# The last pass of a decode-layer gradient kernel, put into written order on each engine

## The chip, the cores and the metric

The kernel runs on one core of a Trainium2 chip. The metric is the device time of one execution in microseconds (us); less is better. "Before" is the kernel as it stands, "after" the kernel with the change. Engines are named as in the profile: PE (matmul; PEld is its weight load), DVE (vector), ACT (scalar), POOL and SP. POOL and SP mostly issue DMAs here.

## What is computed

Two decode steps of a layer pair run one after the other on a single token and share all weights and caches: grouped-query attention over a cache of 65,536 positions, then a two-layer perceptron with a squared ReLU. The kernel returns the output and the gradients of everything.

```python
x = x + A(layernorm(x), k_cache, v_cache, wq, wo)   # 4 KV groups, 8 query heads each, head size 128
x = x + B(layernorm(x), w1, b1, w2, b2)             # relu(x @ w1 + b1) ** 2 @ w2 + b2
x = x + A(layernorm(x), k_cache, v_cache, wq, wo)   # the same caches and weights again
x = x + B(layernorm(x), w1, b1, w2, b2)
out, vjp = jax.vjp(f, ...); grads = vjp(grad_out)   # gradients of x, both caches, wq, wo, w1, b1, w2, b2
```

The caches hold 67 MB each (bf16). Their gradients, as large again, are sums over the two uses, so they can only be written in the last pass, when the scores and the upstream gradients of both uses are known.

## The kernel before

The kernel goes over the caches in four passes: forward attention of the first use, forward of the second, backward of the second (`attn_bwd3`, query gradient only) and a last pass, `attn_bwd4` (line 1050). The last pass does the backward of the first use and writes the cache gradients of both. It takes about the last 765 us of the span and is what the change touches.

**Items and units.** The last pass works on 4 groups of 64 *items*. An item is 8 columns of a group, 8 blocks of 128 positions by 128 numbers, 0.26 MB of K and 0.26 MB of V; it produces as much gradient of each. Four items make a *unit* of 32 columns. For each item i there are these stages:

- `vT` (L1100): 8 PE transposes of V into a PSUM tile `ps_tr`, and one evacuation (copy from PSUM to SBUF by ACT or DVE, lines 155 and 158 in the helper `evac`).
- `vS` (L1123, the "products"): 8 matmuls of the transposed V with the upstream gradients into `ps_sc`. At a unit's first column a matmul subtracts a correction (L1114). At its last column DVE multiplies twice by the exponentials (L1132, L1133), POOL copies twice (L1134, L1135), and the four parts are the tile X.
- `xT_behind` (L1149): once per unit, 8 PE transposes of X and one evacuation.
- `k8`: `dq` (L1166), 8 matmuls of K with X, then `grads` (L1194), two pairs of matmuls, here called A and B. Each fills a `ps_gg` tile with 1,024 fp32 columns, which ACT or DVE evacuates into a staging area. After four items POOL issues the two gradient writes (L1214, L1215).

`ps_tr` and `ps_gg` have two buffers each, `ps_sc` has one.

**Background steps.** A table `bg` holds steps that are due at a loop count. In the last pass they are: row dot products (`dot_va`: a DVE multiply at L433, then an ACT sum at L434 that needs it), which fetch 0.26 MB each; weight gradients; and set-ups of the next group. A weight gradient comes as *rows* steps (L1245 two small DVE casts, L1248 four small matmuls into `ps_gg`, one evacuation) and *out* steps (`outer2`, L1275: two matmuls into `ps_gg`, one evacuation, and per two steps a 0.5 MB write by POOL, L1279). Nearly every loop count from 73 to 226 has one rows or out step: 38 rows and 116 out steps. The rows steps come in five stretches (9, 9, 6, 10 and 4 of them).

**Order.** A scheduler arranges each engine's instructions at build time by priority and its own idea of when their inputs are ready; at run time each engine keeps that order. A helper `in_order` (line 640) runs a step and ties the first instruction that it adds on each engine behind the one written before it on that engine, without a wait between engines; with `each=True` it ties every one. `pipeline` (line 659) walks the loop count i, calls each stage for item i minus its lag, then the background steps of i under `in_order`. In the last pass (line 1232) the stages are free to be moved and of each background step only the first instruction per engine is tied. The opening, up to items 13, 11, 8 and 6 of the stages, is written out by hand and tied instruction by instruction. Which engine takes an evacuation is decided by a running sum of estimated costs at the time the line is written.

K and V tiles are fetched by SP (L284, 1 MB per four items) into a ring of SBUF areas; a fetch waits until the area's last reader on PE is done. An evacuation into a staging area waits until that area's previous write has landed.

Of the kernel before, what the change touches and what calls it, by code (L numbers as in the profile page):

```python
# [18 lines left out]
def kernel(  # L19
# [24 lines left out]
    nc = tc.nc  # L44
    NOSYNC = mybir.DependencyInfo(mybir.DependencyClass.NoSync, mybir.DependencyReason.DATA)
# [21 lines left out]
    UB4 = 512 // R2  # L67
    IPG = C // 8
    TLEAD = 2
# [119 lines left out]
    def part(ap, i, n):  # L189
        return ap[:, i * n:(i + 1) * n]  # L190
# [449 lines left out]
    def in_order(fn, each=False):  # L640

        insts = nc.cur_bb.bb.instructions
        n0 = len(insts)
        before = {}
        fn()
        new = list(insts[n0:])
        want = {i.engine for i in new}
        k = n0 - 1
        while want - set(before) and k >= max(0, n0 - 4000):
            before.setdefault(insts[k].engine, insts[k])  # L650
            k -= 1
        for i in new:
            p = before.pop(i.engine, None)
            if p is not None:
                tc.add_manual_dep(i, p.name, NOSYNC, reason="in_order")
            if each:
                before[i.engine] = i

    def pipeline(n, stages, bg=None, done=()):
        maxlag = max(l for _, l in stages)  # L660
        for i in range(n + maxlag):
            for k, (fn, lag) in enumerate(stages):
                if (done[k] if done else 0) <= i - lag < n:
                    fn(i - lag)
            for fn in (bg or {}).pop(i, ()):
                in_order(fn)
        assert not bg, sorted(bg)

    def items_of(order, turn=0):
# [50 lines left out]
    def attn_fwd(L, order, eT, s_areas, more=None, keep=(), have=(), q_at=(20, 4), narrow=None):  # L720
# [80 lines left out]
        def v8(idx):  # L801
# [9 lines left out]
            if c8 + 8 == C:  # L811
                sl = slice(g * R, (g + 1) * R)
                nc.vector.tensor_tensor(out=L["oT"][:, sl], in0=ps_o[:, :, 0], in1=L["rZ"][:, sl], op=ALU.mult)
                nc.vector.tensor_copy(out=L["oTb"][:, sl], in_=L["oT"][:, sl])

        pipeline(n, [(kT, 0), (kS, TLEAD), (v8, LAGV)], bg)
        return vstream.areas

# [161 lines left out]
    def attn_bwd3(L, og, order, eT, dqT, bg, turn, vhad):  # L980
# [49 lines left out]
        def k8(idx):  # L1030
# [13 lines left out]
            if idx % IPG == IPG - 1:  # L1044
                nc.vector.scalar_tensor_tensor(out=dqT[:, g * R:(g + 1) * R], in0=ps_dq[:, 0, :], scalar=SCALE,
                                               in1=L["rZ"][:, g * R:(g + 1) * R], op0=ALU.mult, op1=ALU.mult)

        pipeline(n, [(vT, 0), (vS, TLEAD), (k8, TLEAD + UB // 8 + 1)], bg)

    def attn_bwd4(La, Lb, oga, ogb, order, eTa, eTb, dqT, bg, group_done, streams, more_stage, tail, KT, vts):  # L1050
        lname = "B1"
        kit = items_of(order)
        n = len(kit)
# [175 lines left out]
        assert len(vts) == 3 and UB4 == 4 * 8  # L1229
        for fn, *args in opening:  # L1230
            in_order(lambda: fn(*args), True)
        pipeline(n, [(vT, 0), (vS, TLEAD), (xT_behind, TLEAD), (k8, TLEAD + UB4 // 8 + 1)], bg, (13, 11, 8, 6))


    def rows_into(rows, cols, nj, twice=False):
# [190 lines left out]
    bg = {}  # L1426
# [136 lines left out]
    stages = Turn([part(e, i, OG) for i in range(2) for e in e_first] + [area[5][:, SLOT - OG:SLOT]])  # L1563
# [31 lines left out]
    bg = {}  # L1595
# [8 lines left out]
    done = [IPG * (j + 1) + LAG4 + 1 for j in range(G)]  # L1604
# [22 lines left out]
    def the_end():  # L1627
        PS["end"] = True
        with tc.high_priority():
# [5 lines left out]
    last_tasks = gwq_tasks(ORD4[-1:], False)  # L1635
    after = [2, 0, 0, 1, 1, 1, 1, 1]
    attn_bwd4(L1, L3, og1, og3, ORD4, eT1, eT3, dqT1, bg, group_done, streams, more_stage,
              lambda i: [t for _, t in zip(range(after[i]), last_tasks)], KT4, vts)
    PS["last"] = True
# [34 lines left out]
```

## Time and profile before

| | before |
|---|---|
| median of 3 runs | 1965.01 us (1962.03 to 1968.48) |
| the profiled execution's own time | 1966.73 us |
| its span | 1965.0 us |
| busy in the span: PE, PEld, DVE, ACT, POOL | 81%, 67%, 56%, 52%, 11% |
| moved by DMA | 802.40 MB, mean 408 GB/s |
| last pass, 1200 to 1965 us: busy PE, DVE, ACT | 619 us, 572 us, 546 us of 765 us |

The span is one execution on the core; the time around it is 1.7 us. "DMA share" is the mean busy share of the core's 16 DMA engines, and "PEclk" the share of full clock that PE was granted. A row of the chain or of the waits gives the engine and line that waited, then what ended the wait.

### The profile page before, as it was taken

What the parts mean: (1) busy time and instruction counts of PE and PEld (TensorE: products, weight loads), DVE (VectorE), ACT (ScalarE), POOL (GpSimd) and SP (SyncE); (2) the same over time, 40 slices, a digit from 0 to 9 for tenths busy, and PEclk for the clock granted to TensorE, in tenths of its full rate; (3) what the DMA queues carried; (4) which work ended last, traced back from release to release, by engine and by line L of the source; (5) the groups of instructions that cost most, each with busy time, mean ns of one, the idle gap of its engine ahead of it and who ended that gap; (6) DMA issues with size and microseconds to landing.
All of it is one profiled execution on the core that took longest, in us unless ns stands there. A gap on an engine that the chain in (4) does not pass through costs nothing. (4 is left out here: it accounts for less than half of the span.)

```text
span 1965.0 us, 65956 instructions
## 1 busy us (share of the span) xinstructions
PE 1582.4 (81%) x30001; PEld 1311.4 (67%) x30052; DVE 1102.6 (56%) x1827; ACT 1028.8 (52%) x1302; POOL 209.5 (11%) x374
## 2 busy tenths in 40 slices
PE   7887887579788866887869888788878688887886
PEld 6887786579788766877868776555555455555553
DVE  4544431046344313746454537687868688776776
ACT  3543433044433322535454437677776677677675
POOL 0000000000000000000000002223222222222222
PEclk9999997669998976899999989899999899999997
DMA  9999999989999999999999999999999999999998
GB/s 395 425 423 421 414 409 404 412 335 421 425 420 420 424 408 391 421 417 419 417 416 402 404 404 409 363 412 420 423 422 422 347 419 422 422 420 421 414 419 328
DMA packets 116227, 802.40 MB, mean 408 GB/s; under 512 B 11484, under 2 KB 11498, under 8 KB 58090
## 3 DMA queue, kind: packets, MB, share of 16 engines
q1 hardware_dynamic: 77530, 612.54, 75.5%
q0 software_dynamic: 30352, 170.94, 21.1%
q10 hardware_dynamic: 8064, 14.68, 2.0%
q8 instruction: 235, 3.85, 0.8%
q14 instruction: 46, 0.38, 0.0%
HBM read 628.18 MB, written 169.95 MB: 406 GB/s over the span
## 5 line engine op out<-in xcount | busy, mean ns | idle before, releaser
L158 DVE COPY small<-ps_tr 128x1024 bf16<-128x1024 bf16 x630 | 427.4, 688 | 315.2 <-PE ps_tr L747 176.5
L155 ACT COPY small<-ps_tr 128x1024 bf16<-128x1024 bf16 x375 | 376.1, 1014 | 360.5 <-PE ps_tr L747 206.9
L155 ACT CAST pair<-ps_gg 128x1024 bf16<-128x1024 f32 (+2 forms) x275 | 264.2, 974 | 119.6 <-PE ps_gg L1194 77.2
L158 DVE CAST pair<-ps_gg 128x1024 bf16<-128x1024 f32 (+1 forms) x209 | 246.8, 1182 | 95.1 <-PE ps_gg L1194 67.1
L747 PE MATMUL ps_tr<-ident_b,pair 128*128 128x128 bf16 x3328 | 252.1, 226 | 38.9 <-DMA pair<-in_A_k_cache_dram 28.3
L1194 PE MATMUL ps_gg<-pair,small 64*128 64x512 bf16 x1024 | 200.1, 399 | 57.1 <-DVE pair L158 15.9
L747 PEld LDWEIGHTS <-pair 128*128 128x128 bf16 x3328 | 201.3, 101 | 44.6 <-DMA pair<-in_A_k_cache_dram 31.8
L809 PE MATMUL ps_acc<-eT,pair 128*128 128x64 bf16 x3840 | 169.3, 205 | 42.8 <-DMA pair<-in_A_v_cache_dram 38.5
L1100 PE MATMUL ps_tr<-ident_b,pair 128*128 128x128 bf16 x2024 | 179.9, 226 | 14.0 <-DVE small L158 5.9
L766 PE MATMUL ps_sc<-L_qpad,small 128*128 128x64 bf16 (+7 forms) x3456 | 174.5, 195 | 18.4 <-ACT small L155 10.9
L809 PEld LDWEIGHTS <-pair 128*128 128x128 bf16 x3840 | 152.9, 104 | 46.3 <-DMA pair<-in_A_v_cache_dram 41.6
L1100 PEld LDWEIGHTS <-pair 128*128 128x128 bf16 x2024 | 127.9, 101 | 69.7 <-issue 59.6
L766 PEld LDWEIGHTS <-small 128*128 128x128 bf16 x3456 | 141.2, 100 | 29.7 <-ACT small L155 17.0
L434 ACT ACTIVATE pair<-pair 128x1024 bf16<-128x1024 bf16 (+1 forms) x105 | 118.5, 1131 | 47.0 <-DVE pair L433 46.9
L1194 PEld LDWEIGHTS <-small 64*128 64x128 bf16 x1024 | 58.7, 94 | 108.8 <-issue 79.5
L999 PE MATMUL ps_tr<-ident_b,pair 128*128 128x128 bf16 x1536 | 120.4, 227 | 11.6 <-DMA pair<-in_A_v_cache_dram 5.6
L155 ACT CAST eT<-ps_gg 128x1024 bf16<-128x1024 f32 (+1 forms) x102 | 101.9, 1005 | 45.7 <-PE ps_gg L1275 15.1
L999 PEld LDWEIGHTS <-pair 128*128 128x128 bf16 x1536 | 95.3, 102 | 30.4 <-issue 19.0
L1123 PE MATMUL ps_sc<-DOB,small 128*128 128x64 bf16 (+3 forms) x2048 | 113.3, 196 | 2.3 <-ACT small L1545 1.2
L1020 PE MATMUL ps_sc<-B_dOpad,small 128*128 128x64 bf16 (+7 forms) x2048 | 104.1, 194 | 13.6 <-DVE small L158 6.3
L1123 PEld LDWEIGHTS <-small 128*128 128x128 bf16 x2048 | 88.5, 100 | 36.9 <-issue 30.0
L1166 PE MATMUL ps_acc<-small,pair 128*128 128x64 bf16 (+1 forms) x2048 | 107.3, 194 | 0.4
(293 smaller groups left out, 2059.2 us busy)
## 6 DMA issues: line engine op xcount, KB each, us to landing
pair<-in_A_v_cache_dram SPq DMA_DIRECT2D x74, 2048.0 KB, 19.4
pair<-in_A_k_cache_dram SPq DMA_DIRECT2D x63, 2048.0 KB, 20.0
out_dram<-pair POOLq DMA_DIRECT2D x100, 1024.0 KB, 20.5
pair<-in_A_v_cache_dram SPq DMA_DIRECT2D x80, 1024.0 KB, 12.2
pair<-in_A_k_cache_dram SPq DMA_DIRECT2D x78, 1024.0 KB, 11.7
eT<-in_A_k_cache_dram SPq DMA_DIRECT2D x21, 2048.0 KB, 20.8
eT<-in_A_v_cache_dram SPq DMA_DIRECT2D x12, 2048.0 KB, 27.1
out_dram<-eT POOLq DMA_DIRECT2D x41, 512.0 KB, 24.2
```

What stands on the lines that cost most here:

```text
L155: nc.scalar.copy(out=out, in_=in_)
L158: nc.vector.tensor_copy(out=out, in_=in_)
L434: nc.scalar.activation(out=view, in_=view, func=ACTF.Copy, accum_out=ycol)
L747: nc.tensor.transpose(pt[:, i, :], kb8[:, i, :], ident_b[:, :])
L766: nc.tensor.matmul(ps_s[:, slot:slot + w, :].rearrange("p a b -> p (a b)"), lhsT=kt[:, i, :], rhs=L["qpad"][:, g, 0:w, :].rearrange("p a b ...
L809: nc.tensor.matmul(ps_o[:, :, :].rearrange("p a b -> p (a b)"), lhsT=vb8[:, i, :], rhs=eT[g][:, :, c:c + 8], start=(c == 0), stop=(c == C ...
L999: nc.tensor.transpose(pt[:, i, :], vb8[:, i, :], ident_b[:, :])
L1020: nc.tensor.matmul(ps_dp[:, slot:slot + w, :].rearrange("p a b -> p (a b)"), lhsT=vt[:, i, :], rhs=dOpad[:, g, 0:w, :].rearrange("p a b -> ...
L1100: nc.tensor.transpose(pt[:, i, :], vb8[:, i, :], ident_b[:, :])
L1123: nc.tensor.matmul(ps_dp[:, slot:slot + w, :].rearrange("p a b -> p (a b)"), lhsT=vt[:, i, :], rhs=DOB[:, g, 0:w, :].rearrange("p a b -> p ...
L1166: nc.tensor.matmul(ps_dq[:, 0:w, :].rearrange("p a b -> p (a b)"), lhsT=kb8[:, i, :], rhs=X[:, sl:sl + w, :].rearrange("p a b -> p (a b)") ...
L1194: nc.tensor.matmul(pg[:, t2 * 512:(t2 + 1) * 512], lhsT=xt[64 * t2:64 * t2 + 64, blk0 + half, :], rhs=GG[64 * t2:64 * t2 + 64, :, :, :].re ...
```

## The change

`pipeline` gets an argument `hold`. With `hold=1` every instruction of a background step is tied behind the one before it on its engine, and every instruction of the next loop count's stages is tied behind the last background instruction on its engine. The last pass calls `pipeline` with `hold=1`. A wrapper `held` ties every instruction of each stage in the order in which it is written, except for the last four items. The stages are listed in another order, V transposes, `k8` (dq and gradients), X transposes, products; X transposes get one more loop count of lag. Nothing is added to or taken from the computation.

On PE the changed kernel then has, for each item from the opening to the end: 8 V transposes, 8 dq, 4 gradient matmuls, once per unit 8 X transposes and the correction, 8 products, the background step. Before, the same stretch has orders such as "2 gradient matmuls, 4 V transposes, 2 out, 4 V transposes, 8 products".

```diff
-    def pipeline(n, stages, bg=None, done=()):
+    def pipeline(n, stages, bg=None, done=(), hold=0):
         maxlag = max(l for _, l in stages)
+        insts = nc.cur_bb.bb.instructions
+        walls = []
         for i in range(n + maxlag):
+            n0 = len(insts)
             for k, (fn, lag) in enumerate(stages):
                 if (done[k] if done else 0) <= i - lag < n:
                     fn(i - lag)
+            for new in list(insts[n0:]):
+                for _, wall in walls:
+                    if new.engine in wall:
+                        tc.add_manual_dep(new, wall[new.engine].name, NOSYNC, reason="behind")
+            n0 = len(insts)
             for fn in (bg or {}).pop(i, ()):
-                in_order(fn)
+                in_order(fn, hold > 0)
+            if hold:
+                wall = {x.engine: x for x in insts[n0:]}
+                walls = [(j, w) for j, w in walls + [(i, wall)] if j > i - hold and w]
         assert not bg, sorted(bg)
...
-        pipeline(n, [(vT, 0), (vS, TLEAD), (xT_behind, TLEAD), (k8, TLEAD + UB4 // 8 + 1)], bg, (13, 11, 8, 6))
+
+        def held(fn):
+            return lambda idx: in_order(lambda: fn(idx), True) if idx < n - 4 else fn(idx)
+        pipeline(n, [(held(vT), 0), (held(k8), TLEAD + UB4 // 8 + 1), (held(xT_behind), TLEAD + 1), (held(vS), TLEAD)], bg, (13, 6, 8, 11), 1)
```

Lines after `pipeline` stand 11 lower in the changed kernel, those after the end of `attn_bwd4` 14 lower.

## The prediction

> **What bounds the kernel now.** I looked at the windows view by stretch first (columns: length; busy time and count of PE, PEld, DVE, ACT, POOL; granted clock; DMA share; GB/s).
>
> ```profile
> 1290.00:1450.00 160.00, 135.85 (x1952) 91.04 (x1959) 125.31 (x187) 122.35 (x139) 43.24 (x70) 0.98 1.01 421
> ...
> 1250.00:1290.00 40.00, 32.20 (x448) 21.91 (x448) 27.15 (x34) 27.47 (x31) 8.07 (x15) 0.87 0.90 356
> 1520.00:1580.00 60.00, 43.03 (x473) 25.82 (x478) 39.10 (x62) 40.60 (x49) 12.75 (x23) 0.86 0.93 360
> 1930.00:1965.00 35.00, 20.65 (x225) 10.25 (x222) 21.01 (x49) 15.75 (x29) 7.49 (x14) 0.66 0.74 289
> ...
> 1580.00:1700.00 120.00, 99.84 (x1309) 65.91 (x1320) 96.94 (x133) 90.21 (x110) 31.08 (x56) 0.97 1.02 421
> 1700.00:1880.00 180.00, 149.27 (x1804) 96.31 (x1822) 132.37 (x195) 129.42 (x147) 44.26 (x76) 0.95 1.02 419
> ```
>
> The last pass is bound by its transfers: 16 DMA engines are full (1.01, 1.02) at 419 to 421 GB/s while PE, DVE and ACT have 15 to 30% left. An item moves 4 x 0.262 = 1.049 MB, at 421 GB/s 2.49 us. The trace agrees: from the X copies at 1294.76 to those at 1446.34 there are 15 units, 60 items, 2.53 us each. With an out step an item moves 1.311 MB, 3.11 us; with a row fetch every third item, three take 4.194 MB, 9.96 us. So order can win only where the DMA is not full: at 360 GB/s the 60 us around 1520 to 1580 lose 60 x (1 - 360/421) = **8.7 us**; 1250 to 1290 loses 40 x (1 - 356/421) = 6.2 us; then there is the end.
>
> Next, what the compute side waits for (waits of 1445 to 1880 us, then the DMA issues of the last pass: count, size, median us to landing).
>
> ```profile
> DVE pair L158 <- DMA out_dram<-pair: 11.4, 2, 5.9
> ...
> PE ps_gg L1248 <- DVE r_cc L1245: 6.5, 11, 1.6
> ...
> PE ps_gg L857 <- DVE dlt_prod L855: 3.1, 1, 3.1
> ```
>
> ```profile
> out_dram<-pair POOLq DMA_DIRECT2D x100, 1024.0 KB, 20.5
> ...
> out_dram<-pair POOLq DMA_DIRECT2D x8, 256.0 KB, 6.1
> ```
>
> Evacuations stop for a staging area whose write has not landed: compute is ahead. A gradient write needs 20.5 us, a small one 6.1, so up to about 14 us of work is queued in the DMA. I call this the cover: compute may fall behind by that much before the DMA runs dry (an estimate, since size accounts for part of the 14). The dip of 8.7 us is such a case, right behind a staging wait of 5.5 us and the 3.1 us set-up wait.
>
> **The change part by part.** Its instructions, DMAs and bytes are the same. In the built order POOL's and ACT's DMAs keep their sequence, and SP swaps six neighbouring pairs of K and V fetches, 1 MB against 1 MB: cost 0. On POOL the X copies, for which it now waits 127 us in all for dq to free a buffer, with gradient writes queued behind, come three items after that buffer is free: those waits go, worth nothing while the DMA is full, and at most part of the 8.7 us where it is not. What changes besides is how fast the compute side can go. Step costs from the timeline at full clock, as distance to the next start: 8 V transposes 0.44, 8 dq 0.25, a gradient pair 0.33 (ends after 0.39), 8 products 0.23, out 0.43, rows 0.32, 8 X transposes 0.44, correction 0.32.
>
> ```profile
> 1602.10 0.38 PE L1275 MATMUL ps_gg<-pair 128*128 128x512 bf16 x1
> ...
> 1602.64 0.40 PE L1166 MATMUL ps_acc<-small,pair 128*128 128x64 bf16 x8
> ...
> 1604.33 0.38 PE L1123 MATMUL ps_sc<-DOB,small 128*128 128x64 bf16 x8
> ...
> 1604.74 0.61 DVE L1132 TENSOR_TENSOR small<-ps_sc,eT 128x256 bf16<-128x256 f32 x1
> ...
> 1601.03 1.98 ACT L155 CAST pair<-ps_gg 128x1024 bf16<-128x1024 f32 x2 [0.48 <-PE ps_gg L1194]
> ...
> 1607.64 1.06 ACT L434 ACTIVATE pair<-pair 128x1024 bf16<-128x1024 bf16 x1
> ```
>
> An evacuation of `ps_gg` takes ACT 1.01 (0.95 in a row), DVE 1.22 (1.14 in a row); of `ps_tr` DVE 0.60; X takes DVE 2 x 0.52, the dot DVE 0.60 and ACT 1.06. Semaphores add 0.04 to 0.05 on each side.
>
> *Items without background* (13 to 72, 227 on). PE's steps sum to 0.44 + 0.25 + 0.66 + 0.23 + (0.44 + 0.32)/4 = 1.77 us against 2.49. Before has nearly this order there already. Cost 0; cover: the DMA.
>
> *Out items.* Now A, B and out use the two `ps_gg` buffers close together: out must wait until A is evacuated, and the next A comes after out, 8 V transposes and 8 dq. The ring is A 0.39 + evacuation 1.10 (DVE 1.32) + out 0.43 + 0.44 + 0.25 = 2.61 to 2.83 us; B, products, X transposes and correction fit in its wait. That is 0.3 to 0.5 below the 3.11 of the DMA: hidden.
>
> *Out items with a dot.* On ACT the sum (L434) waits for DVE's multiply, which is tied behind DVE's evacuation, and the out evacuation is tied behind the sum. I walked three items with the dot in the first: there A on ACT ends at 2.08, B on DVE at 2.62, multiply 3.25, sum 4.35, out evacuation 5.30; the next B waits for that, the next out starts at 5.91, the third at 9.05, and three items take 9.5 us. With out on DVE they take 9.0, with X ahead of the dot about 10.4. Against 9.96: cover regained 0.15 per item.
>
> *Rows items.* The casts (L1245) are now tied behind all that DVE has in that item, and PE's rows matmuls, with the next V transposes behind them, wait for the casts. By what DVE holds ahead, the next item starts at 2.45 (V evacuation only), 3.3 (B: 2.59, casts 2.9, rows to 3.27), 3.55 (A and X's evacuation) or 4.3 (B, two X multiplies to 3.63, casts 3.93): 13.6 us per unit against 4 x 2.49 = 9.96, so 0.9 per item and 38 x 0.9 = 34 us behind in all. In the trace of before this wait is 6.5 us in all.
>
> *Group set-ups.* The chain dot, L855, L857, L859 and on, then L1067 to L1088, stays between items: the 3.1 us wait of before and some 1.4 more, 4.5 us, taken as three times.
>
> *First dip and end.* At 1250 SP issues no fetch for 20 us after the ring has lost two areas; that is not changed. The last four items stay free. Cost 0 for both, bounds -6 to 0 and 2 either way.
>
> *Sum*, stretch by stretch, cover at most 14: rows -8 leaves 6; 27 out items +4: 10; rows -8 and set-up -4.5: **2.5 lost**; 32 items +5, rows -5: 0; 16 items +2, rows -9: **7 lost**; after that 41 items, mostly without dots, give back more than the rest takes. About 9.5 us are lost where before loses 8.7: +1. With the granted clock at 0.94, its mean from 1450 to 1880, the ring's 1.51 us of PE become 1.61, the cover grows by 0.1 less per item, and the same count gives 17 lost: +8. The middle is **+5 us**: 1966.7 + 5 = 1971.7 on the scale of the profiled execution (span 1965.0, around it 1.7), and 1970 on that of the median, which lies 1.7 lower.
>
> **The rivals.**
>
> *The dip goes.* Before's dip comes from a scheduled order in which PE stood for the set-up with products, transposes and gradients queued in awkward turns, and POOL held writes behind X copies. If the plain order falls less behind at rows and set-ups than I count, the DMA stays full from 1290 to the end: -8.7, 1966.7 - 8.7 - 1.7 = 1956. For it: before's wait for casts is only 0.6 us each time. Against: in order, the casts stand behind up to 2.6 us of DVE work. It decides at a DMA share of 1.0 in the 60 us around the second group's end.
>
> *Nothing is regained.* If out items run at the pace of the DMA or slower (evacuations of V and X on the wrong engine), the 34 + 13 us are covered by 14 alone: 33 lost, 24 more than before, 1989.
>
> *PE falls to half clock.* The granted clock was 0.55 in the 10 us from 1260, after 10 us in which PE was busy for 5.75; it was 1.00 where PE was busy for 6.6 of 10 (1770 to 1780). In written order an out item keeps PE for about 2.1 of 3.11 us, with one wait of 0.5 to 0.8 us each, near that edge. At half clock the trace has 8 V transposes at 0.83 and 8 dq at 0.52 (1260.47, 1261.70), a pair ending after 0.61; with out doubled to 0.86 the ring is 0.61 + 1.10 + 0.86 + 0.83 + 0.52 = 3.92, 0.81 over the DMA, times 116 items 94 us: 2059.
>
> ```profile
> 1260.47 1.03 PE L1100 MATMUL ps_tr<-ident_b,pair 128*128 128x128 bf16 x8
> 1261.30 0.56 PE L1123 MATMUL ps_sc<-DOB,small 128*128 128x64 bf16 x8
> ```
>
> [...] The trace speaks against it so far, as waits of 0.3 to 0.6 us at 1616 to 1618 left the clock at 1.00.
>
> *The change does not do what it says* is excluded: the built order of PE, DVE and ACT has it item by item.
>
> **How the numbers follow.** Rows and set-ups cost about what the dip costs now: 0.46, own range 1962 to 1980 (0.26 of it within 0.3%, 0.18 slower, 0.02 faster). The dip goes: 0.30 (0.27 faster, 0.03 same). Nothing regained: 0.19, slower. Half clock: 0.05, slower. Together faster 0.29, same 0.29, slower 0.42; 0.3%, 5.9 us, is about what a measurement of this kernel can tell from no change. The range 1954 to 1990 leaves out the half clock, the upper part of the third case and the lower end of the second.
>
> **What would show it.** Right: DMA share under 1.0 in the 50 us around rows stretches two and four, more than 20 us of PE waits for the casts (L1248, then L1262), out waiting for ACT's evacuation of A in most items, no granted clock under 0.9 over a rows stretch. Wrong: waits for casts as short as before, or a full DMA across the second group's end (then the dip goes); or a unit of plain out items over 12.5 us with the DMA not full (then my ring is too short).

## The result and the profile after

The changed kernel takes **1993.85 us** (median of 4 runs, 1989.32 to 1997.95) beside 1964.65 us for the kernel before on the same chip: a ratio of 1.0147, 95% interval 1.0119 to 1.0174, or 29.2 us. The profiled execution has a span of 1992.5 us. The last pass begins near 1200 us in both traces (the first correction matmul starts at 1202.54 and 1201.38 us), so all of the difference lies in it.

The same windows as before (columns: length; busy time and count of PE, PEld, DVE, ACT, POOL; granted clock; DMA share; GB/s), now of the kernel after:

```profile
1250.00:1290.00 40.00, 33.13 (x491) 23.09 (x489) 30.40 (x38) 29.77 (x36) 9.05 (x16) 0.90 0.95 367
1290.00:1450.00 160.00, 125.14 (x1744) 84.11 (x1748) 118.41 (x175) 112.17 (x129) 38.60 (x63) 0.93 0.99 409
...
1520.00:1580.00 60.00, 44.13 (x513) 28.90 (x520) 40.89 (x69) 36.29 (x43) 11.10 (x20) 0.86 0.84 312
1580.00:1700.00 120.00, 90.70 (x1172) 60.73 (x1187) 88.93 (x120) 87.69 (x106) 29.46 (x53) 0.97 0.99 397
1700.00:1880.00 180.00, 136.49 (x1789) 91.10 (x1808) 129.12 (x198) 122.18 (x133) 41.20 (x73) 0.96 0.98 396
```

The column to read is the last one. Where the kernel before moved 419 to 421 GB/s, this one moves 396 to 409, and 312 in the dip. In those three stretches PE, DVE and ACT are busy for less of the window too, and in no window is one of them full: the transfers wait for the compute side, and the compute side waits for itself. The waits of 1445 to 1880 us name it (who waited, what ended it: us in total, times, longest):

```profile
PE ps_gg L1262 <- DVE r_cc L1259: 34.4, 23, 2.8
...
ACT pair L434 <- DVE pair L433: 26.2, 18, 3.0
...
PE ps_gg L1289 <- DVE pair L158: 18.9, 31, 1.6
...
PE ps_gg L1289 <- ACT pair L155: 15.1, 25, 1.9
...
PE ps_gg L868 <- DVE dlt_prod L866: 6.2, 2, 3.2
```

The same waits of the kernel before, but for the casts (6.5 us, shown in the prediction):

```profile
ACT pair L434 <- DVE pair L433: 7.2, 7, 1.7
...
PE ps_gg L1275 <- DVE pair L158: 5.6, 10, 0.8
...
PE ps_gg L1275 <- ACT pair L155: 4.2, 11, 0.9
```

The wait for the casts is now PE's longest, the dot sum's wait for its multiply has more than tripled, and out's waits for an evacuation by DVE or ACT have grown from 5.6 and 4.2 us to 18.9 and 15.1. The evacuations that stopped for a write still in flight, 27.1 us on ACT and DVE before, have shrunk to 1.2, and the gradient writes land sooner:

```profile
out_dram<-pair POOLq DMA_DIRECT2D x100, 1024.0 KB, 12.8
```

12.8 us where it was 20.5: by my estimate less is queued up in the DMA, whose share in the long windows is 0.98 or 0.99 where it was 1.01 or 1.02. Both fit a kernel whose bound has moved from the transfers to the compute side; the runs without the writes, below, test that.

For finer counts I use the distance between the correction matmuls (L1114, now L1125), one per unit of four items. Three stretches matter: units 0 to 18, units 18 to 57 (the part with rows and out steps) and units 57 to 63.

| us | units 0-18 | units 18-57 | units 57-63 |
|---|---|---|---|
| before | 166.6 | 503.2 | 56.1 |
| after | 168.7 | 533.9 | 55.3 |

30.7 us of the difference is in units 18 to 57, the part with nearly all of the background matmuls.

**Two places in the trace.** First a rows step of the kernel after (start, duration, engine, line, operation; in brackets the idle time ahead and what ended it):

```profile
1378.93 1.22 DVE L158 CAST pair<-ps_gg 128x1024 bf16<-128x1024 f32 x1
1380.07 0.58 DVE L1143 TENSOR_TENSOR small<-ps_sc,eT 128x256 bf16<-128x256 f32 x1
1380.57 0.59 DVE L1144 TENSOR_TENSOR small<-ps_sc,eT 128x256 bf16<-128x256 f32 x1
1381.07 0.24 DVE L1259 CAST r_cc<-L_g 128x4 bf16<-128x4 f32 x2
...
1381.36 0.38 PE L1262 MATMUL ps_gg<-ident_b,r_cc 128*2 128x128 bf16 x4 [2.17 <-DVE r_cc L1259]
```

The casts are 0.24 us of work that needs nothing from this item. In written order they stand behind an evacuation and both X multiplies, and PE, with the next V transposes behind the rows matmuls, is idle for 2.17 us. Then a dot sum at a unit's end:

```profile
1537.18 0.60 DVE L1143 TENSOR_TENSOR small<-ps_sc,eT 128x256 bf16<-128x256 f32 x1
...
1537.70 0.58 DVE L1144 TENSOR_TENSOR small<-ps_sc,eT 128x256 bf16<-128x256 f32 x1
1538.20 0.68 DVE L433 TENSOR_TENSOR pair<-pair 128x1024 bf16<-128x1024 bf16 x1
1538.92 1.06 ACT L434 ACTIVATE pair<-pair 128x1024 bf16<-128x1024 bf16 x1 [2.35 <-DVE pair L433]
...
1539.98 0.56 ACT L155 CAST eT<-ps_gg 128x512 bf16<-128x512 f32 x1
...
1540.59 0.39 PE L1205 MATMUL ps_gg<-pair,small 64*128 64x512 bf16 x2 [2.61 <-ACT eT L155]
```

Here the wait runs through three engines. ACT stands 2.35 us at the sum because DVE's multiply is behind X; the evacuation of out stands behind the sum although its matmuls were done long before; and PE waits 2.61 us for the buffer that this evacuation frees.

### The profile page after: what moved, and what is told of

Its sections match the earlier page's. It is cut to its first block, busy times and chain, and to the rows that moved or that the text cites. A ratio compares the mean times of both kernels' runs of the same rounds, so it can differ in the third digit from the quotient of the medians.

```text
span 1992.5 us, 65943 instructions
## 1 busy us (share of the span) xinstructions
PE 1567.2 (79%) x29994; PEld 1306.3 (66%) x30052; DVE 1108.6 (56%) x1824; ACT 1034.9 (52%) x1305; POOL 207.9 (10%) x374
## 5 line engine op out<-in xcount | busy, mean ns | idle before, releaser
L158 DVE CAST pair<-ps_gg 128x1024 bf16<-128x1024 f32 x205 | 243.7, 1190 | 73.8 <-PE ps_gg L1205 50.8
L758 PE MATMUL ps_tr<-ident_b,pair 128*128 128x128 bf16 x3328 | 250.3, 224 | 41.8 <-DMA pair<-in_A_k_cache_dram 31.7
L1205 PE MATMUL ps_gg<-pair,small 64*128 64x512 bf16 x1024 | 189.1, 401 | 45.7 <-ACT pair L155 11.0
L1111 PE MATMUL ps_tr<-ident_b,pair 128*128 128x128 bf16 x2024 | 162.4, 226 | 5.4 <-DMA pair<-in_A_v_cache_dram 1.8
L777 PEld LDWEIGHTS <-small 128*128 128x128 bf16 x3456 | 139.0, 99 | 29.7 <-ACT small L155 17.1
L434 ACT ACTIVATE pair<-pair 128x1024 bf16<-128x1024 bf16 (+1 forms) x105 | 118.4, 1129 | 72.3 <-DVE pair L433 72.0
L1010 PE MATMUL ps_tr<-ident_b,pair 128*128 128x128 bf16 x1536 | 119.1, 225 | 11.6 <-DMA pair<-in_A_v_cache_dram 5.5
L1134 PEld LDWEIGHTS <-small 128*128 128x128 bf16 x2048 | 76.9, 100 | 76.5 <-issue 76.5
L155 ACT CAST eT<-ps_gg 128x1024 bf16<-128x1024 f32 (+1 forms) x99 | 97.4, 987 | 36.7 <-PE ps_gg L1289 13.9
L1205 PEld LDWEIGHTS <-small 64*128 64x128 bf16 x1024 | 48.2, 94 | 100.0 <-issue 82.4
L1134 PE MATMUL ps_sc<-DOB,small 128*128 128x64 bf16 (+3 forms) x2048 | 105.7, 196 | 1.2 <-ACT small L1559 1.2
## 6 DMA issues: line engine op xcount, KB each, us to landing
out_dram<-pair POOLq DMA_DIRECT2D x100, 1024.0 KB, 12.8
eT<-in_A_k_cache_dram SPq DMA_DIRECT2D x21, 2048.0 KB, 18.9
out_dram<-eT POOLq DMA_DIRECT2D x41, 512.0 KB, 12.8
```

The source lines that it names most:

```text
L155: nc.scalar.copy(out=out, in_=in_)
L158: nc.vector.tensor_copy(out=out, in_=in_)
L434: nc.scalar.activation(out=view, in_=view, func=ACTF.Copy, accum_out=ycol)
L758: nc.tensor.transpose(pt[:, i, :], kb8[:, i, :], ident_b[:, :])
L777: nc.tensor.matmul(ps_s[:, slot:slot + w, :].rearrange("p a b -> p (a b)"), lhsT=kt[:, i, :], rhs=L["qpad"][:, g, 0:w, :].rearrange("p a b ...
L1010: nc.tensor.transpose(pt[:, i, :], vb8[:, i, :], ident_b[:, :])
```

## The experiments

My theory after this reading: the written order makes the compute side itself slower than the transfers, by three costs: casts, dot sums, and the ring through the two `ps_gg` buffers. Rivals: the new stage order alone, or the ties alone, or lost overlap with the writes.

**Which half of the change.** `walls_only` keeps before's free stages and list and adds only `hold=1`; `held_only` keeps the held stages in the new order and leaves `hold` out.

```diff
-        pipeline(n, [(held(vT), 0), (held(k8), ...), (held(xT_behind), TLEAD + 1), (held(vS), TLEAD)], bg, (13, 6, 8, 11), 1)
+        pipeline(n, [(vT, 0), (vS, TLEAD), (xT_behind, TLEAD), (k8, ...)], bg, (13, 11, 8, 6), 1)      # walls_only
+        pipeline(n, [(held(vT), 0), ..., (held(vS), TLEAD)], bg, (13, 6, 8, 11))                       # held_only
```

> Stages in their old order and free to be moved, background steps tied instruction by instruction and kept between the loop counts. If the tied background steps (rows steps waiting for casts, dots, set-ups) cause the loss, nearly all of it stays: 1985 to 1995 us, with over 30 us of PE waits for the casts. If the fixed order of the stages causes it, most of it goes: 1964 to 1972.

> Stages in the new order and tied, background steps as in the kernel before: only the first instruction of a step on each engine tied, and nothing kept behind the step but what the tied stages themselves keep. As every stage is tied behind what is written before it, the background steps end up between the items all the same. Theory of tied background steps: still slow, 1980 to 1995, if the ties of the stages alone keep the steps in their place; the theory that the wall is what counts expects 1965 to 1972.

Measured: `walls_only` 2022.45 us, ratio 1.0278 (1.0247 to 1.0308); `held_only` 1990.63 us, 1.013 (1.0105 to 1.0154), and its interval overlaps that of the full change. So the held stages alone do what the change does, and the walls add nothing that can be told once the stages are tied. The walls on the old list are worse still, above both of my forecasts for that run. Its PE waits in the last pass:

```profile
PE ps_gg L1262 <- DVE r_cc L1259: 39.3, 30, 2.3
PE ps_gg L1289 <- ACT pair L155: 38.4, 43, 2.3
...
PE ps_tr L1160 <- DVE small L1144: 33.3, 43, 1.6
```

The third line stands out: with the X transposes right behind the products, PE waits for X. In the change, where they come one loop count later, the same wait is 9.2 us, and in the kernel before, which may move them, 15.6. POOL's X copies also wait 206.4 us for dq here, 152.6 before and 5.4 in the change. Which of these makes `walls_only` the slowest I have not tried.

**Each wait by itself.** `rows_ahead` does the casts of a rows step one background step earlier; `sums_later` does the sum (L434) one loop count behind its multiply, with the fetch one later too, so that its areas last. `rows_sums` has both.

```diff
+        def casts(j0):        # the two DVE casts of a rows step, called by the step before
...
+                step.ahead = lambda j0=j0: casts(j0)
...
+        if t + 1 < len(tasks) and hasattr(tasks[t + 1], "ahead"):
+            at(bg, i0 + t * (i1 - i0) // len(tasks), tasks[t + 1].ahead)
```

```diff
+                    nc.vector.tensor_tensor(out=view, in0=view, in1=vbc, op=ALU.mult)
+                    return
...
+            def two(k):
+                nc.scalar.activation(out=view, in_=view, func=ACTF.Copy, accum_out=...)
...
+                    at(bg, i0 + k * step + 1, lambda k=k: two(k))
```

> The changed kernel, with the two casts of a rows step done at the end of the background step before it, for all but the four rows pieces that are laid out twice. Theory that the casts cause most of the loss: PE's wait for them falls from 45 us to under 10 and the time by 12 to 22 us, to 1972 to 1982. Theory that the ring through the two ps_gg buffers limits every item with a background step: the wait moves to the ring and the time falls by under 6 us.

> The changed kernel, with the ACT sum of each row dot product one loop count after the DVE multiply (its fetch comes one count later, so that the buffer is free). Theory that the dots cause a good part: ACT's wait for the multiply falls from 37 us to under 10 and the time by 8 to 15 us, to 1979 to 1986. Theory that only rows steps and set-ups matter: under 4 us.

> The changed kernel with both mends, casts one step ahead and ACT sums one loop count later. Each alone took 22 us off. If each of them leaves the compute side just fast enough for the DMA, they do not add up: 1955 to 1968 us, the time that the full DMA sets. If the two costs lie beside each other and simply add, minus 44: 1950. If the ring through the two ps_gg buffers still limits the out items, 1966 to 1972.

| | us | ratio (95%) | units 18-57 |
|---|---|---|---|
| `rows_ahead` | 1972.34 | 1.0032 (1.0016 to 1.0048) | 507.4 |
| `sums_later` | 1971.35 | 1.0038 (1.002 to 1.0055) | 505.6 |
| `rows_sums` | 1967.55 | 1.0015 (1.0006 to 1.0023) | 498.4 |

The unit times are those of the profiled executions (1977.77, 1971.56 and 1963.95 us), so they do not follow the medians exactly. In `rows_ahead` PE's wait for casts falls from 44.8 us over the last pass to 4.3 and the dot sum's is still 36.4; in `sums_later` the casts' wait is still 40.7 us and the dot sum's is not among those of 9.9 us and more. Each mend alone takes back about 22 us, both together 26. For the sums that is more than I had forecast (8 to 15). Either the two share a cause, or a floor hides the rest; the time of `rows_sums` lies in two of the ranges that I had set for it and cannot tell. There the writes land after 21.9 us again (20.5 before), at a DMA share of 1.01 from 1290 to 1450 and from 1450 to 1880 us, which points to the transfers as the floor.

**The same mends without the change.** `before_both` is the kernel before with both mends.

> The kernel before with the same two mends, so its order stays with the scheduler. If written order with short chains is the better order, this stays behind the changed kernel with both mends by 4 us or more: 1962 to 1968. If the mends alone are what counts and the DMA sets the time, both give the same within 4 us.

1965.68 us, ratio 1.0005 (0.9995 to 1.0015): no difference. Before waits 7.6 us for casts and 10.9 us for dot multiplies in the whole last pass, and removing these waits gains nothing.

**The compute side alone.** `before_nowrite` and `after_nowrite` leave the writes of the cache gradients out, except for the first 16 and the last 8 items, so most of the cache gradients is not returned. Each ran once.

```diff
             elif j0 + 8 == J:
-                nc.gpsimd.dma_start(out=half_of(GKv[g], b), in_=st[:, 0, :, :])
-                nc.gpsimd.dma_start(out=half_of(GVv[g], b), in_=st[:, 1, :, :])
+                pass
```

> Leaves out the writes of the cache gradients in the last pass, but for the first 16 and the last 8 items, so the DMA has some 120 MB less to move and the compute side runs at its own pace. From the catch-up stretch of the kernel before (9 us per unit) the 153 loop counts with rows and out steps should take about 2.3 to 2.5 us each, the whole some 1770 to 1810.

> The changed kernel with the same writes left out. If the written order is slower on the compute side, as the walked items say (2.6 to 2.8 us for an out item, 3.0 to 3.2 with a dot every third, 3.4 for rows), its 153 loop counts take about 3.0 to 3.2 us each, 70 to 110 us more than the kernel before without those writes. If the loss came from the transfers, the two would differ by under 30 us.

1922.86 us for the order of before, 1993.68 us for the written order. The windows from 1450 to 1850 us, first of `after_nowrite`:

```profile
1450.00:1850.00 400.00, 304.91 (x3841) 200.57 (x3841) 284.65 (x417) 271.07 (x311) 58.90 (x103) 0.93 0.66 230
```

and of `before_nowrite`:

```profile
1450.00:1850.00 400.00, 343.43 (x4395) 220.33 (x4395) 321.70 (x471) 306.46 (x361) 67.88 (x113) 0.98 0.73 260
```

The written order is no faster with a third of the DMA idle. Its units 18 to 57 take 535.4 us without the writes and 533.9 with them. This settles the bound: **the compute side alone sets the 1994 us**, and the order costs it 1993.7 - 1922.9 = 70.8 us, at the low end of the 70 to 110 that I had expected. The kernel before, 1963.41 us in the same session, has 41 us of slack under its transfers, which hide that much; the rest, 30, is about what was measured. My number for `before_nowrite` itself, 1770 to 1810, missed by over 110 us: the compute side of before is much nearer to its transfers than I thought. The granted clock in these two rows is 0.93 and 0.98, so a part of the 70.8 us may come through a lower clock; the runs do not divide it.

Where the slack lies matters. Units 0 to 18 take 165.6 us without the writes and 166.6 with them, so these writes do not set the pace there in the kernel before either; units 18 to 57 take 467.8 against 503.2, which is 35.4 of the 41 us.

**The ring.** `split` keeps everything of the change but sets the two gradient pairs of an item apart: dq and A, V transposes, B, X transposes, products. A, B and out then use the two `ps_gg` buffers at more even distances.

```diff
-        pipeline(n, [(held(vT), 0), (held(k8), TLEAD + UB4 // 8 + 1), (held(xT_behind), TLEAD + 1), (held(vS), TLEAD)], bg, (13, 6, 8, 11), 1)
+        LAGK = TLEAD + UB4 // 8 + 1
+        pipeline(n, [(held(kA), LAGK), (held(vT), 0), (held(kB), LAGK), (held(xT_behind), TLEAD + 1), (held(vS), TLEAD)], bg, (6, 13, 6, 8, 11), 1)
```

> The changed kernel, but the two gradient pairs of an item no longer stand side by side: dq and A, then the V transposes, then B, X transposes, products, background step. The three users of the two ps_gg buffers (A, B, out) are then spread over the item. Ring theory (the out items have nothing to give back because A, B and out stand close together on two buffers): the out items fall from 2.95 to 3.15 us to about 2.5 to 2.7, the debts of the rows steps and dot sums are paid back, time 1968 to 1980, units 18 to 57 in 505 to 520 us. Rival (the casts and dot sums alone set the pace, the buffers do not matter): within 6 us of the changed kernel's 1994, units 18 to 57 at 534.

> The split order with the cache-gradient writes left out except those of the first 16 and the last 8 items of a group pass, so part of the cache gradients is not returned: the pace of the compute side alone. The changed kernel without these writes took 1993.7. Ring theory: 1950 to 1975, units 18 to 57 in 490 to 515 us against 535. Rival (casts and dot sums alone): 1984 or more.

`split` measured 1994.06 us, 1.0156 (1.0137 to 1.0176): no gain, and here the ring theory's number missed. `split_nowrite` took 1980.19 us, 13.5 less than `after_nowrite` but 5 above the range that I gave. By stretch, units 18 to 57 fell from 535.4 to 515.6 without the writes and from 533.9 to 522.3 with them, while units 0 to 18 rose by 8.3 and 4.2 us and, with the writes, units 57 to 63 by 6.8. The latter is mostly one stall of 5.74 us at 1922.70, of PE behind two evacuations that waited for a staging area's write:

```profile
1921.40 1.01 ACT L155 CAST eT<-ps_gg 128x1024 bf16<-128x1024 f32 x1 [4.29 <-DMA out_dram<-eT]
1921.42 1.22 DVE L158 CAST eT<-ps_gg 128x1024 bf16<-128x1024 f32 x1 [6.40 <-DMA out_dram<-eT]
```

So the distances between the three users of the buffers are a cost where the out steps are, and the same split costs time where they are not. Why this stall falls there in `split` and not in the others, I have not tried.

**One cost or three.** The two mends together gave less than their sum; without the writes the transfers hide nothing. Four more kernels, one run each, all with the writes left out as above.

> The changed kernel with the casts of a rows step one background step ahead and with the cache-gradient writes left out except those of the first 16 and the last 8 items (part of the cache gradients is not returned): what the casts cost the compute side, not capped by the transfers. The changed kernel without these writes took 1993.7, units 18 to 57 535 us. Separate costs (casts, dot sums and the ring each cost their own time): 25 to 35 us less, units 18 to 57 at 500 to 510. Rival (one wait hides the other, and removing one only lengthens the next): under 12 us less with the writes gone too; then the 22 us that this mend gave with the writes in place would have come from elsewhere.

> The changed kernel with the dot sum one loop count later and the same writes left out. Separate costs: 22 to 32 us less than 1993.7, units 18 to 57 at 503 to 513. Rival (one wait hides the other): under 12 us less.

> The changed kernel with both mends and the same writes left out. Separate costs: 45 to 65 us less than 1993.7, units 18 to 57 at 470 to 490; then the sum of the two mends with writes, 26 instead of 44, was capped by the transfers. Rival (the two mends take away the same time): 22 to 30 us less, units 18 to 57 at 505 to 513.

> Both mends and the gradient pairs of an item apart, the same writes left out. If the ring through the two ps_gg buffers still costs after the casts and sums are mended: 10 to 25 us below the two mends alone. If it no longer does (A, B and out were late only because of the sums and casts ahead of them): within 6 us of the two mends alone.

| without the writes | us | units 0-18 | units 18-57 |
|---|---|---|---|
| `after_nowrite` | 1993.68 | 166.4 | 535.4 |
| `rows_nowrite` | 1971.37 | 166.5 | 512.0 |
| `sums_nowrite` | 1963.04 | 169.7 | 505.3 |
| `both_nowrite` | 1931.49 | 166.0 | 478.1 |
| `split_nowrite` | 1980.19 | 174.7 | 515.6 |
| `split_both_nowrite` | 1933.54 | 180.1 | 460.5 |
| `before_nowrite` | 1922.86 | 165.6 | 467.8 |

Casts 22.3 us (a little under my 25 to 35), sums 30.6, both 62.2: separate costs that add up. Both together come out 9 us above the sum, but these are single runs from different sessions, and the changed kernel alone spreads over 8.6 us; in units 18 to 57 it is 57.3 against 53.5. The 26 us of `rows_sums` were capped by the transfers: without its writes the same kernel takes 1931.49 us, with them 1967.55. In units 18 to 57 the split takes off 19.8 us without the mends and 17.6 with them: a third, separate cost. But the total of the two mends does not fall with the split (1933.54 against 1931.49), because units 0 to 18 give 14 us back. My number for that run was wrong by total and right by stretch.

**Is there a better version?** `split_rows_sums` has the split and both mends; `split_all` also spreads each group set-up over more loop counts.

> The split order with both mends: casts of a rows step one background step ahead, dot sum one loop count later. If all three waits are what the written order costs, the transfers alone are left: 1955 to 1967, last-pass waits for casts, dot multiplies and evacuations of A all short. If the ring does not matter, the same as the two mends without the split, 1967.5 within 3.

> As the one before, and each group set-up is spread over more loop counts (product, sums, casts and turn in steps of their own), so that PE does not stand through the chain of a set-up. If the set-ups (about 8.9 + 5.9 us of waits over three) are what still opens a gap in the transfers: 3 to 8 us below the one before, 1953 to 1963, which would beat the kernel before. If the transfers cover them: within 2 us of it.

1972.01 us, 1.0035 (1.0023 to 1.0048), and 1965.97 us, 1.0005 (0.9996 to 1.0015). Neither beats the kernel before. `split_rows_sums` missed both of its forecasts: its units 18 to 57 take 489.7 us, less than the 498.4 of `rows_sums`, but units 0 to 18 take 178.2 against 165.6. Spreading the set-ups took 6 us off, as forecast if they still opened a gap. With `rows_sums` and `before_both`, three of four differently ordered kernels end within 0.2% of it, and the fourth 0.35% above: once the compute side is out of the way the transfers set about the same time, and no order changes their bytes.

## Why the prediction failed, point by point

It said 1970 us and the kernel takes 1994. The direction was that of the forecast, the size was that of the rival "nothing is regained" (1989). Two terms of the sum failed: the out items give no cover back, and the rows items cost more than was counted.

- **What bounds the kernel now: right.** Before, the transfers bind. How far above its own pace the compute side stood I took from a queue (the cover of about 14 us); `before_nowrite` has it as 41 us over the whole pass. A cover is refilled only as fast as the new order's compute outruns the transfers, and that was the step that failed.
- **Items without background, POOL, SP: cost right, pace not.** Units 0 to 18 and 57 to 63 moved by +2.1 and -0.8 us. An item takes the compute side 2.1 to 2.2 us there (units 7 to 11 of after, 8.4 to 8.7 us each), not the 1.77 of PE's steps. POOL's waits of X copies for dq fell from 152.6 us over the whole last pass to 5.4, and were worth nothing.
- **Out items: the step that failed.** I counted a ring of 2.61 to 2.83 us, which would regain 0.3 to 0.5 us per item. Units 47 to 52, out steps with neither rows nor dots, took 75.7 us, 3.15 per item, against 3.11 for the transfers: nothing regained. Without the writes they take 75.3, so this is the compute side's own pace. The trace shows the ring itself:

```profile
1803.72 0.59 PE L1289 MATMUL ps_gg<-pair 128*128 128x512 bf16 x2 [0.53 <-DVE pair L158]
...
1805.40 1.21 DVE L158 CAST pair<-ps_gg 128x1024 bf16<-128x1024 f32 x1
...
1806.67 0.38 PE L1289 MATMUL ps_gg<-pair 128*128 128x512 bf16 x1 [0.53 <-DVE pair L158]
...
1807.10 0.61 PE L968 MATMUL ps_tr<-ident_b,pair 128*128 128x128 bf16 x8
...
1809.82 0.38 PE L1289 MATMUL ps_gg<-pair 128*128 128x512 bf16 x1 [0.54 <-ACT pair L155]
```

  From out to out it is 2.95 us with A on DVE, 0.12 over my upper end (dq alone takes 0.32 us to the next start there, not 0.25), and 3.15 with A on ACT, where eight weight transposes (L968, 0.45 us to the next start) stand in the background step. I had left these out: a step costs all that it issues. But units 47 and 48 have no weight transposes and still take 3.07 per item. At a unit's last item (out at 1785.59, next out at 1788.76, 3.17 us) out does not wait for A at all: the X transposes and the correction, which I had put into the ring's wait, keep PE at work for all but 0.16 us of it. The structure was right for the other items (out does wait for A, with 0.53 and 0.54 us), the size was not, and so little separates the ring from the transfers that 0.2 us decides. `split` agrees: units 47 to 52 fall to 72.5, and without the writes from 75.3 to 68.8.
- **Dot triples: near in size, but the gain was not there.** Units 20 to 25 took 82.8 us, with a set-up in unit 24. Without that unit it is 66.3 us for 20 items, 9.94 per three; units 31 to 36, with neither rows nor set-up, took 77.7, 9.71 per three. I had 9.5 and the transfers 9.96, so 0.01 to 0.08 us per item were regained where I counted 0.15. The dot sum's wait cost the compute side 30.6 us (`sums_nowrite`), of which about 10 lie in such units (20 to 25, 31 to 36, 39 to 41) and most of the rest where dots meet rows steps and set-ups, a meeting that I had not priced.
- **Rows items: right in mechanism, too cheap.** I gave 13.6 us per unit. The first unit of rows alone, from 1370.09 to 1383.55, took 13.5, but the seven units that are all rows (18, 27, 28, 37, 43, 44, 53; most have a dot or weight transposes besides) took 14.9 on average. That is 47 us over the transfers' pace for 38 rows, not 34; the waits for the casts are 44.8 us in the last pass. Moving the casts takes off 22.3 (`rows_nowrite`).
- **Group set-ups: near.** The three units with one (12, 24 and 30) took 4.6, 3.5 and 6.9 us more than the mean of their neighbours, 15.0 in all, where I had 13.5. PE's waits in their chains (L868, L1093) are 14.8.
- **Sum.** By these counts the rows lose 47 and the set-ups 15, the cover gives 14 and out items and dots about 3 where I had over 11. That leaves 45 lost, 36 more than before, which is 2001 us: 7 above the measurement. The 14 us of cover, taken from a queue, may be the term that is short; no run shows it.
- **The dip goes: wrong.** From 1520 to 1580 the DMA moves 312 GB/s, a loss of 60 x (1 - 312/421) = 15.5 us instead of 8.7. By units the transfers run dry at rows steps (27 and 28) and at the set-up of unit 30, and are full over the plain out items (47 to 52; columns as in the windows above):

```profile
1497.20:1527.86 30.66, 20.76 (x277) 13.49 (x275) 19.51 (x40) 18.18 (x22) 4.54 (x8) 0.89 0.84 328
1541.70:1561.80 20.10, 13.81 (x131) 8.82 (x132) 13.05 (x32) 10.24 (x12) 3.31 (x6) 0.67 0.74 272
...
1775.64:1851.36 75.72, 62.12 (x819) 42.49 (x830) 55.36 (x65) 55.90 (x58) 19.92 (x36) 0.99 1.02 413
```

- **PE falls to half clock: did not come.** The mean granted clock from 1450 to 1880 us is 0.94 in both kernels. In units 47 to 52 out waits for an evacuation about 0.5 us at a time in 18 of 24 items (9.7 us in all, the longest 0.8), and the clock was 0.99 all the same. The edge that I had put between 5.75 and 6.6 us of busy PE in 10 us was an estimate from stretches of the trace of before. I counted PE busy for 2.1 of 3.11 us in an out item, near that edge; it was busy for 62.12 of 75.72 us here, so this stretch does not test it.
- **The signs.** DMA share under 1.0 around rows stretches and over 20 us of waits for casts came. Out does wait for evacuations, but 80 times over 116 steps, and for DVE's (43) more often than ACT's (37). The clock went just under 0.9 in two rows stretches (0.89). "A unit of plain out items over 12.5 us with the DMA not full" was the sign of a ring too short a count: half of it came, 12.6 us at a DMA share of 1.02. That the ring was too short a count is shown by the run without the writes instead.

What stays open: how the 29 us divide among casts, sums, ring and set-ups with the writes in place. The costs sum to more than 29, and the transfers hide a part that depends on the order in which they come.

## What to carry to other kernels

When a kernel is bound by its transfers, measure how much faster its compute side is (leave a transfer out) before pricing a reordering: that slack (41 us here), and not a queue's length (14 us), says what an order may cost. In a written order look for short operations that need nothing new, like a cast of 0.16 us, and for sums that wait for another engine, and put each a step away from what it would wait for. Where a forecast rests on a pace that beats the bound by 5 to 15%, list every instruction of the step and work out the slower engine's case, since the sign hangs on it.

## What was not expected of the hardware

Nothing new in kind. In numbers: the costs of two waits that cross engines added up (22.3 and 30.6 us alone, 62.2 together, single runs), and a kernel with 25% of PE, 28% of DVE and 32% of ACT idle from 1450 to 1880 us (321.86, 309.89 and 294.33 us busy of 430) was bound by none of them and not by its DMA, only by the order in which they wait for each other.
